# Dealing the routing of 24 token tiles to other places in a recurrence with a mixture of experts behind it

## The chip, the cores and the metric

One core of a Trainium2 chip runs the whole program. The metric is the device time of one execution in microseconds; the time of a kernel is the median of its runs.

## The reference, cut to what matters

A linear recurrence ("attention") runs over 4 batches, 8 heads, 768 positions and 48 channels; its output, 3072 rows of 384, goes into a layer of 8 experts with one expert for each row, and only for rows whose skip score is positive.

```python
for t in range(S):
    cur = einsum('bhd,bhe->bhde', u * k[t], v[t])
    y[t] = einsum('bhd,bhde->bhe', r[t], state + cur)
    state = w * state + einsum('bhd,bhe->bhde', k[t], v[t])
x = y.transpose(0, 2, 1, 3).reshape(3072, 384)
do = x @ w_skip > 0
logits = x[do] @ w_gate                  # 8 columns
e = argmax(logits);  g = max of softmax(logits)
out = x;  out[do] += g * (relu(x[do] @ w1[e]) @ w2[e])   # 384 -> 1024 -> 384
```

## The kernel before

The attention works on 24 tiles of 128 rows: two batches by 64 positions, twelve tiles for each pair of batches. A loop of 23 steps (`for n in range(NT - 1)`, L905) makes tile n+1 in step n. All engines execute in the order in which the program issues (the schedule is manual), so the order of the calls in the loop is the order of the work on each engine.

PE in step n: `scores(n + 1)` (L441, into ps_p), `across(n + 1)` (L527, the state's part, from sblk), `turn_k(n + 2)` (L454), `turn_x(n)` (L569, the finished tile transposed for the gate), route matmuls if any, `state(n + 1)` (L474), and `within(n + 1)` (L503), which needs the masked scores am. Every fourth step holds the gate's matmuls for four tiles (`gate_some`, L597, steps 3, 7, ..., 19; the step after it `gate_back`, L613), which give the logits lg.

DVE in step n: the two masks of the scores (L462, L463), then what the routes have for this step, then `prep_r` of tile n+3 (L411, L419) and, every fourth step, the decayed state sblk (L486) between these two. POOL multiplies the keys of tile n+3 (kd, L429) and, from step 7, makes the low half of a piece of the experts' weights (lo, L114); ACT casts its high half (hi, L113) and copies results out of PSUM. SP issues the loads (dm, vz, raw) and the stores of the finished tiles.

A *route* (L634, a generator) turns the logits of a group of tiles into places in the experts' lists. Its groups are tiles 0 to 7, 8 to 15, 16 to 19 and 20 to 23. Its stages, each up to a `yield`: the largest logit and the choice (L646 to L670, one-hot oh); the rank matmuls on PE (L673 to L683, with the running count `before`); the rank arithmetic (L708 to L731); the one-hot of the lane ol and of the slot oj (L778, L782; for the later groups ol alone, L737, with 128 elements for each tile); the values vl (L789 or L744: row id and gate weight in two parts); the matmuls that collect vl by ol into the lists (L796 or L750) and the additions to `lists`. A `yield` of 0 lets a tick take the next stage at any place; 1, 2 and 4 mark stages that begin with PE work, taken at one place in a step. After group 2, `gather` (L122, POOL) fetches the rows of expert 0's first 128 slots from the stored output. The gathered tiles have numbers of their own, and 0 and 8 are expert 0's: where a gather or an expert is spoken of, "tile 0" and "tile 8" are these.

How many stages a step takes is set by `tick`:

```python
tick((1, 1, 2)[n % 3] if n < EARLY else 3 if n < TE else 6)     # EARLY = 16, TE = 20
```

A group starts when its logits are there: group 1 in step 8, group 2 in step 16, group 3 in step 20 (steps 20 and later take further stages at their end, L937 to L942), group 4 behind the loop. Behind the loop stand the transposes of tile 0 (L145), the transposes and gate of the last tile (L569, L613, L581), the first half of expert 0 (`widen`, L194) and, woven into it, the route of group 4, the gather of tile 8, and then the other experts (L154, L164), which run to the end.

Of the kernel before, what the change touches and what calls it, by code (L numbers as in the profile page):

```python
# [9 lines left out]
F32 = mybir.dt.float32  # L10
F32R = mybir.dt.float32r
# [5 lines left out]
ALU = mybir.AluOpType  # L17
AX = mybir.AxisListType
# [3 lines left out]
N, DM, E, F = B * S, H * D, 8, 1024  # L22
P = 128
# [23 lines left out]
EARLY = 16  # L47
# [5 lines left out]
W_MIN, W_MAX = 0.8, 1.2  # L53
HUGE = 1e30
FIRST = 12
GROUPS = [(0, 8), (8, 16), (16, 20), (20, 24)]


@with_exitstack
def tile_wkv_moe(  # L60
# [11 lines left out]
    nc = tc.nc  # L72
# [171 lines left out]
    with ExitStack() as actx:  # L244
# [348 lines left out]
        def gate_some(n, k=GB):  # L593
            pg = ps_l[:, : k * C]
            for j in range(NCC):
                for c in range(2):
                    nc.tensor.matmul(  # L597
                        pg[c * C : (c + 1) * C, :],
                        wgp[:, j, c, :],
                        gts[0][:, j, c, :k, :].rearrange("p k t -> p (k t)"),  # L600
                        start=(j == 0),
                        stop=(j == NCC - 1),
                        skip_group_check=True,
                    )
            lt = turned_lg[n] = wk.tile([P, GB * C], F32, tag="lt", name=f"lt{n}", bufs=1)[:, : k * C]
            nc.scalar.copy(lt, pg)
# [25 lines left out]
        lists = cpool.tile([P, NV3, NJ, E], F32, name="lists")  # L632

        def route(g0, g1):  # L634
            n, late = g1 - g0, g0 >= EARLY
            rp = ps_l if g1 == NT else ps_r
            mine = rp[:, : NV3 * NSL]
            l8 = lg[:, g0:g1, 0:E]
# [3 lines left out]
            def small(tag, dt=F32, w=None, bufs=None):  # L642
                return sm.tile([P, n] if w is None else [P, n, w], dt, tag=tag, name=f"{tag}{g0}", bufs=bufs)
# [16 lines left out]
            df = small("df", w=E)  # L660
            nc.vector.tensor_tensor(df, l8, bc(mx), ALU.subtract)
            yield 0
            if not late:
                nc.scalar.activation(df, df, AF.Exp)
            nc.vector.tensor_tensor(eq[:, :, :E], eq[:, :, :E], rdo, ALU.mult)
            m2 = small("m2")
# [1 line left out]
            yield 0  # L668
            oh = small("oh", BF16, E)
            nc.vector.tensor_tensor(oh, eq[:, :, :E], bc(m2), ALU.is_equal)  # L670
            yield 4 if late else 1
            pr = rp[:, 256:]
            nc.tensor.matmul(pr[:, : n * E], tri, oh.rearrange(col), start=True, stop=False, skip_group_check=True)  # L673
# [8 lines left out]
            for j in range(1, n):  # L682
# [5 lines left out]
                    stop=(j == n - 1),  # L688
                    skip_group_check=True,
                )  # L690
            gw = small("gw")

            def weigh():
                nc.vector.tensor_reduce(gw, df, AX.X, ALU.add)  # L694
                nc.vector.tensor_scalar(gw, gw, 1e-9, None, ALU.add)

            if late:
                nc.scalar.activation(df, df, AF.Exp)
            else:
                weigh()  # L700
            yield 0
            rk = small("rkp", w=E)
            gh, gl = small("gh", F32R), small("gl", F32R)
            r1 = small("r1")
            sums = sm.tile([P, E], F32, tag="sums", name=f"sums{g0}")

            def ranks():
                nc.vector.tensor_tensor(rk, pr[:, : n * E].rearrange("p (n e) -> p n e", e=E), oh, ALU.mult)  # L708

            def count():  # L710
                nc.vector.tensor_reduce(sums, oh.rearrange("p n e -> p e n"), AX.X, ALU.add)

            if late:
                ranks()
# [21 lines left out]
            if late:  # L736
                nc.vector.tensor_tensor(  # L737
                    ol, lane1[:, None, :].to_broadcast([P, n, P]), r1.unsqueeze(2).to_broadcast([P, n, P]), ALU.is_equal
                )
                vl = small("vl", F32R, NV3 * E)  # L740

                def value(*qs):
                    for q in qs:
                        nc.vector.tensor_tensor(  # L744
                            vl[:, :, q * E : (q + 1) * E], oh, vals[q].to_broadcast([P, n, E]), ALU.mult
                        )

                def collect(v0, v1):
                    for j in range(n):
                        nc.tensor.matmul(  # L750
                            part[:, v0:v1, NJ - 1, :],
                            ol[:, j, :],
                            vl[:, j, v0 * E : v1 * E],
                            start=(j == 0),
                            stop=(j == n - 1),
                        )
                    into = lists[:, v0:v1, NJ - 1, :]
                    nc.vector.tensor_tensor(into, part[:, v0:v1, NJ - 1, :], into, ALU.add)

                value(0)  # L760
                yield 4
                collect(0, 1)
                if g1 == NT:
                    place_ids(1)
                yield 0
                weigh()
                nc.vector.reciprocal(gw, gw)
                nc.vector.tensor_copy(gh, gw)
                nc.vector.tensor_tensor(gl, gw, gh.bitcast(F32), ALU.subtract)
                value(1, 2)  # L770
                if g1 < NT:
                    count()
                    nc.vector.tensor_tensor(before, before, sums, ALU.add)
                yield 4
                collect(1, NV3)
                nc.vector.tensor_scalar(over[:, g0:g1], r1, float(CAP), None, ALU.is_ge)
                return
            nc.vector.tensor_tensor(  # L778
                ol, lane[:, None, :].to_broadcast([P, n, P]), lo.unsqueeze(2).to_broadcast([P, n, P]), ALU.is_equal
            )  # L780
            oj = small("oj", w=NSL)
            nc.vector.tensor_tensor(  # L782
                oj, blk[:, None, :].to_broadcast([P, n, NSL]), hi.unsqueeze(2).to_broadcast([P, n, NSL]), ALU.is_equal
            )
            nc.vector.tensor_tensor(before, before, sums, ALU.add)
            yield 0
            vl = small("vl", F32R, NV3 * NSL)
            for q, val in enumerate(vals):
# [21 lines left out]
        def place_ids(j):  # L810
            nc.vector.tensor_scalar(gid[:, j * E : (j + 1) * E], lists[:, 0, j], 1.0, 0.0, ALU.subtract, ALU.max)
# [6 lines left out]
            nc.vector.scalar_tensor_tensor(sid[:, c], ids, -1.0, em2, ALU.add, ALU.add)  # L818
            nc.vector.tensor_tensor(gate_s[:, c], lists[:, 1, j], lists[:, 2, j], ALU.add)

        ends = {g1: g0 for g0, g1 in GROUPS}
        routes = []

        def step_route(kind):
            if routes and routes[0][1] == kind and routes[0][2] < seen[0] + 2:
                k = next(routes[0][0], None)
                if k is None:
                    routes.pop(0)
                else:
                    routes[0][1] = k  # L830
                return True
            return False

        def tick(k=1):
            for _ in range(k):
                step_route(0)

        def both(g):
            for _ in g:
                pass  # L840
# [32 lines left out]
        def piece(j, split=False):  # L873
            e, j = divmod(j, NPC)
            if split:
                split_piece(e, j, nc.gpsimd)
            else:
                load_piece(e, j)
# [26 lines left out]
        for n in range(NT - 1):  # L905
            if n + 5 < NT:
                load_dm(n + 5)
            if n + 4 < NT and n:
                load_v(n + 4)
            scores(n + 1)  # L910
            mask_scores(n + 1)
            across(n + 1)
            if n >= FIRST_LOAD + LEAD:
                piece(n - FIRST_LOAD - LEAD, split=True)
            if 0 < n and n + 2 < NT:
                bonus(n + 2, BH)
            turn_k(n + 2)
            if 0 < n <= TE and n % GB == 0:
                gate_back(n - 1)
            turn_x(n)  # L920
            if n + 3 < NT:
                prep_k(n + 3)
            for kind in (1, 2, 4):
                step_route(kind)
            tick((1, 1, 2)[n % 3] if n < EARLY else 3 if n < TE else 6)
            if n + 3 < NT:
                prep_r(n + 3, (0,))
            back = state(n + 1)
            if n + 3 < NT:
                prep_r(n + 3, (1,))  # L930
            if n < TE and n % GB == GB - 1:
                gate_some(n)
            elif n == NT - 2:
                gate_some(n, NT - 1 - TE)
            within(n + 1, kcopy.get(n + 2, xcopy[n]))
            evac(n + 1)
            if back:  # L937
                back()
            if n >= TE:
                for kind in (1, 2, 4):  # L940
                    step_route(kind)
                tick()  # L942
            if n + 1 in ends:
                routes.append([route(ends[n + 1], n + 1), 0, n + 1])
            if 1 <= n < 5:
                next(setup, None)
            if n >= FIRST_LOAD:
                piece(n - FIRST_LOAD)
        done = NT - 1 - FIRST_LOAD - LEAD
        for j in range(done + LEAD, 2 * NPC):  # L950
            piece(j)
# [9 lines left out]
        turn_x(NT - 1)  # L961
        piece(done, split=True)
        gate_back(NT - 2, NT - 1 - TE)
        run(1)
        gate(NT - 1)
        last = route(ends[NT], NT)
        while next(last) == 0:
            pass
        run(2)
# [366 lines left out]
```

## Time and profile before

| | |
|---|---|
| median of 3 runs | 274.98 us (274.95 to 278.34) |
| the profiled execution, its own time | 276.32 us |
| its span, first to last instruction | 274.2 us, clock 0.998 |
| PE, DVE, ACT, POOL busy | 255.6, 183.2, 141.1, 131.4 us |
| chain that ended last, by engine | PE 82%, DVE 10%, ACT 3% |

The profile is one execution. Its parts used here are the table of stretches (busy time of each engine between two moments), the instructions of an engine in order of time, with the idle time ahead of each and what ended it in brackets, and the chain of waits that ended last. A line number in a row is that of the kernel before.

### The profile page before, as it was taken

The numbers are of one execution on the slowest core, as the hardware profiler recorded it, in microseconds if no ns is written. First come the engines' busy times: TensorE is split into PE (matmuls) and PEld (weight loads), VectorE is DVE, ScalarE is ACT, GpSimd is POOL, SyncE is SP. The second block draws the span as 40 slices with busy tenths as digits, with TensorE's granted clock in tenths as the row PEclk, the third lists the DMA queues.
The fourth block names the chain that finished last, engine by engine and source line by source line (L and its number), as shares of the span: only waits on it lengthen the run. The fifth ranks groups of instructions, "written<-read, shape, count | busy, mean of one in ns | idle before, by whom it ended". The sixth has DMA issues, their size and how long they took to land.

```text
span 274.2 us, 8740 instructions
## 1 busy us (share of the span) xinstructions
PE 255.6 (93%) x3545; PEld 233.9 (85%) x3545; DVE 183.2 (67%) x372; ACT 141.1 (51%) x316; POOL 131.4 (48%) x131
## 2 busy tenths in 40 slices
PE   7998999999979989788999999999999999999990
PEld 2797897878869877776879999999999999999990
DVE  8786657598896899954655686757748377483310
ACT  2664566667756756434455554717548085480300
POOL 8536313375545538511748853763525535255011
PEclk9999999999999999999999999999999999999999
DMA  7977678878999995435479994694837747100010
GB/s 201 308 197 240 163 203 277 248 247 256 289 274 282 272 284 159 114 93 143 111 254 308 365 379 166 219 317 145 260 121 241 241 142 261 43 4 27 15 35 23
DMA packets 31140, 54.30 MB, mean 198 GB/s; under 512 B 4535, under 2 KB 14412, under 8 KB 31088
## 3 DMA queue, kind: packets, MB, share of 16 engines
q1 hardware_dynamic: 28896, 48.19, 57.2%
q0 software_dynamic: 2048, 5.44, 5.8%
q8 instruction: 30, 0.49, 0.7%
q14 instruction: 22, 0.18, 0.2%
q10 hardware_dynamic: 144, 0.00, 0.0%
HBM read 45.82 MB, written 8.65 MB: 199 GB/s over the span
## 4 chain that ended last, share of the span: by engine, by line
PE 82%; DVE 10%; ACT 3%; issue 2%; DMA 1%; POOL 0%; POOLq 0%; ACTq 0%
PE ps_p L164 11%; PE ps_y L164 11%; PE ps_p L441 8%; PE ps_p L154 5%; PE ps_r L154 5%; PE ps_l L154 5%; PE ps_y L154 5%; PE ps_s L474 5%; PE ps_y L503 5%; PE ps_l L454 4%; PE ps_y L527 3%; PE ps_l L597 3%; PE ps_t L569 3%; PE ps_y L216 2%; PE ps_p L216 2%
## 5 line engine op out<-in xcount | busy, mean ns | idle before, releaser
L114 POOL TENSOR_TENSOR lo<-raw,hi 128x512 fp32r<-128x512 f32 x42 | 57.0, 1358 | 75.3 <-ACT hi L113 55.7
L113 ACT CAST hi<-raw 128x512 fp32r<-128x512 f32 x96 | 55.1, 624 | 0.0
L114 DVE TENSOR_TENSOR lo<-raw,hi 128x512 fp32r<-128x512 f32 x54 | 44.0, 837 | 2.6 <-ACT hi L113 2.3
L429 POOL TENSOR_TENSOR kd<-dm,w_d 128x512 f32<-128x512 f32 x22 | 30.1, 1366 | 14.7 <-DMA dm<-in_dm_dram 13.0
L172 POOL DMA_INDIRECT out_dram<-xg,sid x16 | 17.1, 1067 | 36.4 <-DVE xg L169 25.7
L462 DVE COPY_PREDICATED am<-below,ps_p 128x512 f32<-128x512 int8 x24 | 17.7, 739 | 17.1 <-PE ps_p L441 17.0
L441 PE MATMUL ps_p<-rd,kd 64*64 64x128 f32 x768 | 26.9, 276 | 0.3 <-issue 0.3
L441 PEld LDWEIGHTS ps_p<-rd,kd 64*64 64x64 f32 x768 | 20.9, 132 | 3.2 <-issue 0.7
L158 ACT ACTIVATE hh<-ps_p 128x464 fp32r<-128x464 f32 x7 | 3.9, 559 | 36.9 <-PE ps_p L154 20.1
L122 POOL DMA_INDIRECT xg<-out_dram,gid x16 | 18.2, 1139 | 8.7 <-DVE gw L694 4.0
L503 PE MATMUL ps_y<-vz,am 128*64 128x96 f32 x384 | 20.2, 247 | 2.1 <-DVE am L463 1.5
L503 PEld LDWEIGHTS ps_y<-vz,am 128*64 128x64 f32 x384 | 17.8, 137 | 3.4 <-issue 1.9
L405 ACT ACTIVATE rd<-rd,uw 128x128 f32<-128x128 f32 x52 | 17.8, 395 | 4.9 <-DVE rd L411 4.9
L474 PE MATMUL ps_s<-vz,kt 128*64 128x96 f32 x352 | 19.6, 253 | 0.0
L456 ACT COPY kt<-ps_l 128x512 f32<-128x512 f32 x22 | 12.8, 583 | 12.9 <-PE ps_l L454 12.9
L164 PE MATMUL ps_p<-hi,hh 128*128 128x384 f32 x56 | 19.4, 347 | 0.0
L164 PE MATMUL ps_y<-hi,hh 128*104 128x384 f32 x56 | 18.9, 338 | 0.0
L164 PE MATMUL ps_p<-hi,hl 128*128 128x384 f32 x56 | 18.9, 337 | 0.0
L164 PE MATMUL ps_y<-lo,hh 128*104 128x384 f32 x56 | 18.9, 337 | 0.0
L164 PE MATMUL ps_y<-hi,hl 128*104 128x384 f32 x56 | 18.9, 337 | 0.0
L164 PE MATMUL ps_p<-lo,hh 128*128 128x384 f32 x56 | 18.8, 336 | 0.0
L169 DVE SCALAR_TENSOR_TENSOR xg<-ps_y,gate_s,xg 104x384 f32<-104x384 f32 (+1 forms) x8 | 4.9, 616 | 20.5 <-PE ps_y L164 17.9
(244 smaller groups left out, 693.4 us busy)
## 6 DMA issues: line engine op xcount, KB each, us to landing
raw<-in_w_dram SPq DMA_DIRECT2D x96, 256.0 KB
dm<-in_dm_dram SPq DMA_DIRECT2D x24, 512.0 KB
vz<-in_tok_dram SPq DMA_DIRECT2D x48, 96.0 KB
out_dram<-xt SPq DMA_DIRECT2D x48, 96.0 KB
out_dram<-xt SPq DMA_DIRECT2D x4, 192.0 KB
xg<-out_dram,gid POOLq DMA_INDIRECT x16
out_dram<-xg,sid POOLq DMA_INDIRECT x16
wgp<-in_wgq_dram SPq DMA_DIRECT2D x1, 192.0 KB
```

The lines of the kernel that those rows point to most:

```text
L113: nc.scalar.copy(hi, t)
L114: eng.tensor_tensor(lo, t, hi.bitcast(F32), ALU.subtract)
L122: ins = nc.gpsimd.indirect_dma_start(out=xg, out_offset=None, in_=out[0:rows], in_offset=bass.IndirectOffsetOnAxis(ap=gid[:, q : q + 1], a ...
L154: nc.tensor.matmul(ph, a[:, c, fs], b[:, c, :], start=(k == 0), stop=(k == 3 * NCC - 1))
L164: nc.tensor.matmul(py, a, b[:, f, :], start=(k == 0), stop=(k == 3 * NFC - 1))
L172: ins = nc.gpsimd.indirect_dma_start(out=out, out_offset=bass.IndirectOffsetOnAxis(ap=sid[:, q : q + 1], axis=0), in_=xs.pop(q), in_offset ...
L405: nc.scalar.mul(rd[:, :, 1], rd[:, :, 0], uw[:, hp : hp + 1])
L429: (eng or nc.gpsimd).tensor_tensor(kds[n], d[:, 1], w_d[:, n % NSUB, 1][:, :, None].to_broadcast([DR, NHP, 2, C]), ALU.mult,)
L441: nc.tensor.matmul(ps_p[q * C : (q + 1) * C, a, 2 * hp * C : 2 * (hp + 1) * C], kd[h, hp, q, :], rd[h, hp, q].rearrange("p s c -> p (s c)" ...
L462: nc.vector.copy_predicated(shape(am[n % 2]), below, p[:, :, 0])
L474: nc.tensor.matmul(s[a * C : (a + 1) * C, :, hp * D : (hp + 1) * D], kt[:, hp, a, :], t[:, :, a, hp, :], start=i == 0 and hp == 0, stop=Tr ...
L503: ins = nc.tensor.matmul(place_y(a, c)[:, :, g, :], am[n % 2][:, a, hp * C : (hp + 1) * C], t[:, :, a, hp, :], start=g == 0 and n % NSTEP ...
```

## The change

A table, DEAL, now gives the number of stages for each step; steps that are not in it take none. In the route of the first two groups the slot one-hot oj comes in a stage of its own ahead of the lane one-hot ol. Group 3 (`mid`) leaves the loop's list of routes: its choice, gate weights and counts are issued at the end of step 22, its rank matmuls, ranks, ol and vl behind the gate's `gate_back` after the loop, and its collecting matmuls, three lists at once, after the gate of the last tile, ahead of group 4. The stages at the end of steps 20 and later are gone. Line numbers of the changed kernel are higher by 1 to 12 in these parts.

```diff
+DEAL = {8: 2, 9: 2, 10: 1, 11: 1, 12: 1, 13: 1, 15: 2, 16: 4, 17: 2, 19: 2, 20: 2}
...
         def route(g0, g1):
-            n, late = g1 - g0, g0 >= EARLY
+            n, late, mid = g1 - g0, g0 >= EARLY, EARLY <= g0 and g1 < NT
...
-            if not late:
+            if not late or mid:
                 nc.scalar.activation(df, df, AF.Exp)
...
             nc.vector.tensor_tensor(oh, eq[:, :, :E], bc(m2), ALU.is_equal)
+            if mid:
+                weigh()
+                part_weight()
+                count()
             yield 4 if late else 1
...
                 value(0)
+                if mid:
+                    value(1, 2)
+                    nc.vector.tensor_tensor(before, before, sums, ALU.add)
+                    nc.vector.tensor_scalar(over[:, g0:g1], r1, float(CAP), None, ALU.is_ge)
+                    yield 4
+                    collect(0, NV3)
+                    return
...
-            nc.vector.tensor_tensor(
-                ol, lane[:, None, :].to_broadcast([P, n, P]), lo.unsqueeze(2).to_broadcast([P, n, P]), ALU.is_equal
-            )
             oj = small("oj", w=NSL)
             nc.vector.tensor_tensor(
                 oj, blk[:, None, :].to_broadcast([P, n, NSL]), hi.unsqueeze(2).to_broadcast([P, n, NSL]), ALU.is_equal
             )
             nc.vector.tensor_tensor(before, before, sums, ALU.add)
             yield 0
+            nc.vector.tensor_tensor(
+                ol, lane[:, None, :].to_broadcast([P, n, P]), lo.unsqueeze(2).to_broadcast([P, n, P]), ALU.is_equal
+            )
+            yield 0
...
-        ends = {g1: g0 for g0, g1 in GROUPS}
+        ends = {g1: g0 for g0, g1 in GROUPS if g1 <= EARLY}
+        mid = route(*GROUPS[2])
...
-            tick((1, 1, 2)[n % 3] if n < EARLY else 3 if n < TE else 6)
+            tick(DEAL.get(n, 0))
...
             elif n == NT - 2:
                 gate_some(n, NT - 1 - TE)
+                while next(mid) == 0:
+                    pass
             within(n + 1, kcopy.get(n + 2, xcopy[n]))
...
-            if n >= TE:
-                for kind in (1, 2, 4):
-                    step_route(kind)
-                tick()
...
         gate_back(NT - 2, NT - 1 - TE)
+        while next(mid) == 0:
+            pass
         run(1)
         gate(NT - 1)
-        last = route(ends[NT], NT)
+        both(mid)
+        last = route(*GROUPS[3])
```

What the edits do to the order is shown at three places. The first is DVE from the masks of step 13 on (am is written by the masks, rd by prep_r, sblk by the state's decay). Before:

```order
L462 COPY_PREDICATED am_151<-below,ps_p 128x512
L463 COPY_PREDICATED am_151<-eye,ps_p 128x512
L778 TENSOR_TENSOR ol_1431<-lane,lo_1343 128x1024
L782 TENSOR_TENSOR oj_1433<-blk,hi_1248 128x128
L785 TENSOR_TENSOR before<-before,sums_1243 128x8
L411 TENSOR_TENSOR rd_1436<-dm_1189,w_d 128x8x64
L419 TENSOR_TENSOR rd_1436<-rd_1436,uw 128x4x64
L462 COPY_PREDICATED am_152<-below,ps_p 128x512
L463 COPY_PREDICATED am_152<-eye,ps_p 128x512
L789 TENSOR_TENSOR vl_1517<-oj_1433,id_195 128x8x16
```

Now, from behind the same masks of step 13:

```order
L790 TENSOR_TENSOR oj_1432<-blk,hi_1248 128x128
L793 TENSOR_TENSOR before<-before,sums_1095 128x8
L412 TENSOR_TENSOR rd_1435<-dm_1208,w_d 128x8x64
L420 TENSOR_TENSOR rd_1435<-rd_1435,uw 128x4x64
L463 COPY_PREDICATED am_152<-below,ps_p 128x512
L464 COPY_PREDICATED am_152<-eye,ps_p 128x512
L412 TENSOR_TENSOR rd_1516<-dm_1285,w_d 128x8x64
L487 TENSOR_TENSOR sblk_199<-ps_s,pw 128x384
L420 TENSOR_TENSOR rd_1516<-rd_1516,uw 128x4x64
L463 COPY_PREDICATED am_151<-below,ps_p 128x512
L464 COPY_PREDICATED am_151<-eye,ps_p 128x512
L795 TENSOR_TENSOR ol_1431<-lane,lo_1343 128x1024
```

The lane one-hot of group 1 stood in step 13 ahead of rd and of the next step's masks; it now stands behind the masks of step 15, with the three vl behind it. Group 2's ol moved from step 19 to step 20 in the same way.

The second place is PE in step 21, from its scores to the next step's. Before:

```order
L441 MATMUL ps_p<-rd_1997,kd_1986 64x128 x16
L527 MATMUL ps_y<-sblk_199,rd_1997 64x48 x16
L569 MATMUL ps_t<-ident,xt_2139 128x128 x3
L750 MATMUL ps_r<-vl_2159,ol_2157 128x8 x4
L474 MATMUL ps_s<-vz_130,kt_2073 64x2x48 x8
L503 MATMUL ps_y<-vz_130,am_151 64x2x48 x8
L750 MATMUL ps_r<-vl_2159,ol_2157 128x2x8 x4
L441 MATMUL ps_p<-rd_2119,kd_2083 64x128 x16
```

Now:

```order
L442 MATMUL ps_p<-rd_1992,kd_1979 64x128 x16
L528 MATMUL ps_y<-sblk_199,rd_1992 64x48 x16
L570 MATMUL ps_t<-ident,xt_2105 128x128 x3
L806 LDWEIGHTS ones
L806 MATMUL ps_r<-before,ones 128x8
L808 MATMUL ps_r<-vl_2081,ol_1988 128x48 x8
L475 MATMUL ps_s<-vz_130,kt_2068 64x2x48 x8
L504 MATMUL ps_y<-vz_130,am_151 64x2x48 x8
L442 MATMUL ps_p<-rd_2085,kd_2078 64x128 x16
```

Both collects of group 3 (L750) left the step; the collect of group 2, which stood in step 20, is here instead.

The third place is DVE behind the loop (xhl is the low half of tile 0, rkp and r the ranks, mx the start of group 4's route). Before:

```order
L463 COPY_PREDICATED am_152<-eye,ps_p 128x512
L147 TENSOR_TENSOR xhl_2324<-ps_s,xhl_2324 128x384
L646 MEMSET eq_2353 128x4
L648 TENSOR_REDUCE mx_2355<-lg 128x4
L650 SCALAR_TENSOR_TENSOR rdo_2357<-lg,rev 128x32
```

Now:

```order
L148 TENSOR_TENSOR xhl_2297<-ps_s,xhl_2297 128x384
L721 TENSOR_TENSOR rkp_2321<-ps_r,oh_2257 128x32
L725 TENSOR_REDUCE r_2322<-rkp_2321 128x4
L747 TENSOR_TENSOR ol_2325<-lane_193,r_2322 128x512
L754 TENSOR_TENSOR vl_2327<-oh_2257,id_195 128x4x8
L754 TENSOR_TENSOR vl_2327<-oh_2257,gh_2260 128x4x8
L754 TENSOR_TENSOR vl_2327<-oh_2257,gl_2261 128x4x8
L773 TENSOR_TENSOR before<-before,sums_2262 128x8
L774 TENSOR_SCALAR over<-r_2322 128x4
L768 TENSOR_TENSOR lists<-ps_r,lists 128x3x8
L647 MEMSET eq_2348 128x4
L649 TENSOR_REDUCE mx_2350<-lg 128x4
```

Nine instructions of group 3 stand between tile 0's low half and group 4's first reduction; the last of them, the addition to the lists, is behind four matmuls of PE (L760), which PE has after the gate of the last tile (L582).

More of the change, by code (lines that the diff above doesn't have):

```diff
@@ L670, in route, with weigh, part_weight, count @@
             nc.vector.tensor_tensor(oh, eq[:, :, :E], bc(m2), ALU.is_equal)
+            gw = small("gw")
+            gh, gl = small("gh", F32R), small("gl", F32R)
+            sums = sm.tile([P, E], F32, tag="sums", name=f"sums{g0}")
+            def weigh():
+                nc.vector.tensor_reduce(gw, df, AX.X, ALU.add)
+                nc.vector.tensor_scalar(gw, gw, 1e-9, None, ALU.add)
+            def part_weight():
+                nc.vector.reciprocal(gw, gw)
+                nc.vector.tensor_copy(gh, gw)
+                nc.vector.tensor_tensor(gl, gw, gh.bitcast(F32), ALU.subtract)
+            def count():
+                nc.vector.tensor_reduce(sums, oh.rearrange("p n e -> p e n"), AX.X, ALU.add)
+            if mid:
+                weigh()
+                part_weight()
+                count()
             yield 4 if late else 1
@@ L690, in route @@
                 )
[L691 to L697, printed above, removed]
+            if late and not mid:
                 nc.scalar.activation(df, df, AF.Exp)
-            else:
+            elif not late:
                 weigh()
@@ L702, in route @@
             rk = small("rkp", w=E)
-            gh, gl = small("gh", F32R), small("gl", F32R)
             r1 = small("r1")
-            sums = sm.tile([P, E], F32, tag="sums", name=f"sums{g0}")
             def ranks():
                 nc.vector.tensor_tensor(rk, pr[:, : n * E].rearrange("p (n e) -> p n e", e=E), oh, ALU.mult)
-            def count():
-                nc.vector.tensor_reduce(sums, oh.rearrange("p n e -> p e n"), AX.X, ALU.add)
             if late:
@@ L760, in route @@
                 value(0)
+                if mid:
[5 more added lines that the diff above has]
+                    return
                 yield 4
                 collect(0, 1)
-                if g1 == NT:
-                    place_ids(1)
+                place_ids(1)
                 yield 0
                 weigh()
-                nc.vector.reciprocal(gw, gw)
-                nc.vector.tensor_copy(gh, gw)
-                nc.vector.tensor_tensor(gl, gw, gh.bitcast(F32), ALU.subtract)
+                part_weight()
                 value(1, 2)
-                if g1 < NT:
-                    count()
-                    nc.vector.tensor_tensor(before, before, sums, ALU.add)
                 yield 4
@@ L948, in tile_wkv_moe @@
                 piece(n - FIRST_LOAD)
+        assert not routes
         done = NT - 1 - FIRST_LOAD - LEAD
```

## The prediction

> **What bounds the kernel now.** I read the table of stretches first, cut at the first score matmul (L441) of each step: step n runs from scores(n+1) to scores(n+2), so 71.23 us opens step 13 and 118.99 us step 22; the last two long rows are the stretch behind the attention and the experts. A row gives length, then busy time (and instructions) of PE, weight load, DVE, ACT and POOL, the clock, the DMA share and GB/s.
>
> ```profile
> 53.99:71.23 17.24, 16.23 (x385) 14.16 (x385) 15.36 (x32) 11.94 (x29) 10.24 (x8) 1.00 0.85 260
> 71.23:75.10 3.87, 3.87 (x105) 3.53 (x103) 3.16 (x5) 3.04 (x7) 2.54 (x2) 1.00 0.90 259
> 75.10:80.71 5.61, 4.09 (x105) 3.60 (x103) 5.54 (x11) 2.54 (x6) 3.18 (x2) 1.00 0.92 279
> 80.71:86.68 5.97, 5.97 (x125) 5.33 (x123) 4.52 (x8) 3.81 (x9) 2.53 (x2) 1.00 0.96 291
> 86.68:91.54 4.86, 4.45 (x110) 4.01 (x108) 3.43 (x10) 3.44 (x9) 2.52 (x2) 1.00 0.85 256
> 91.54:95.41 3.87, 3.87 (x106) 3.53 (x104) 3.30 (x6) 3.04 (x7) 2.53 (x2) 1.00 0.97 289
> 95.41:99.50 4.09, 4.09 (x115) 3.88 (x113) 3.82 (x10) 2.56 (x6) 2.53 (x2) 1.00 0.97 290
> 99.50:106.34 6.84, 5.67 (x118) 4.57 (x116) 6.74 (x16) 3.85 (x9) 3.50 (x2) 1.00 0.86 244
> 106.34:112.78 6.44, 5.63 (x124) 5.31 (x122) 6.11 (x24) 3.33 (x8) 4.04 (x3) 1.00 0.35 90
> 112.78:118.99 6.21, 4.87 (x111) 4.19 (x107) 5.63 (x18) 3.36 (x9) 1.70 (x1) 1.00 0.41 108
> 118.99:123.38 4.39, 3.82 (x96) 3.30 (x96) 1.71 (x4) 1.11 (x3) 1.27 (x1) 1.00 0.42 108
> 123.38:144.18 20.80, 19.25 (x119) 15.60 (x117) 10.97 (x38) 9.86 (x25) 9.86 (x9) 1.00 0.57 171
> 144.18:268.00 123.82, 123.78 (x906) 122.02 (x904) 73.92 (x119) 59.21 (x118) 58.65 (x48) 1.00 0.54 181
> 71.23:99.50 28.27, 26.34 (x654) 23.88 (x652) 23.78 (x46) 18.42 (x44) 15.83 (x12) 1.00 0.93 278
> ```
>
> PE sets the end. From 144.18 us it works 123.78 of 123.82 us at full clock, so the experts can't shrink, only start earlier. Before them a step without route work takes 3.87 us (steps 13 and 17). Steps 14 and 19 to 21 have PE idle, and there DVE is the fullest engine (5.54 of 5.61, 6.74 of 6.84, 6.11 of 6.44, 5.63 of 6.21). Next I read PE's order of time for what ends those idles (the bracket: idle time before the row, and its releaser).
>
> ```profile
> 60.58 0.88 PE L503 MATMUL ps_y<-vz,am 128*64 128x96 f32 x16 [0.54 <-ACT kt L456]
> 79.90 0.88 PE L503 MATMUL ps_y<-vz,am 128*64 128x96 f32 x16 [1.52 <-DVE am L463]
> 101.77 0.81 PE L527 MATMUL ps_y<-sblk,rd 64*64 64x48 f32 x32 [1.17 <-DVE sblk L486]
> 112.58 0.18 PE L673 MATMUL ps_r<-oh,tri 128*128 128x32 bf16 x1 [0.40 <-DVE oh L670]
> 115.86 0.61 PE L750 MATMUL ps_r<-vl,ol 128*128 128x8 f32 x4 [1.06 <-DVE vl L744]
> 118.45 0.61 PE L750 MATMUL ps_r<-vl,ol 128*128 128x16 f32 x4 [0.20 <-DVE vl L744]
> ```
>
> All come from route work in front of something PE needs: the masked scores (am) at 79.90, the decayed state (sblk) at 101.77, the route's own operands in steps 20 and 21. The cause of the longest is in DVE's and POOL's rows.
>
> ```profile
> 73.67 1.30 POOL L429 TENSOR_TENSOR kd<-dm,w_d 128x512 f32<-128x512 f32 x1
> 73.81 2.24 DVE L778 TENSOR_TENSOR ol<-lane,lo 128x1024 fp32r<-128x1024 f32 x1
> 79.65 0.28 DVE L789 TENSOR_TENSOR vl<-oj,id 128x128 fp32r<-128x128 f32 x1
> 79.84 0.29 DVE L789 TENSOR_TENSOR vl<-oj,gh 128x128 fp32r<-128x128 f32 x1
> 113.95 0.69 DVE L737 TENSOR_TENSOR ol<-lane,r 128x512 fp32r<-128x512 f32 x1
> 114.06 1.70 POOL L114 TENSOR_TENSOR lo<-raw,hi 128x512 fp32r<-128x512 f32 x1 [1.34 <-ACT hi L113]
> 114.56 1.25 DVE L744 TENSOR_TENSOR vl<-oh,id 128x32 fp32r<-128x32 bf16 x1
> ```
>
> The lane one-hot ol starts beside POOL's kd (over at 74.97) and ends at 76.05, 1.08 us after it: it hardly advanced meanwhile. In the last two rows a vl of 32 elements takes 1.25 us and ends at 115.81, just behind POOL's 115.76. The two engines exclude each other here.
>
> **Steps 9 to 12.** The first group's rank matmuls move from step 11 to step 10. They cost 0.22 us, the excess of step 18 (4.09) over step 17 (3.87), and in step 10 stand in the 0.54 us that PE waits for kt: -0.2.
>
> **Steps 13 to 18.** The ol leaves step 13; step 14 loses its wait and falls from 5.61 to 3.87: -1.74. The lists' matmuls (L796) go from step 15 to 16, the second ranks from 18 to 17: no net change. What the eight list matmuls cost a step is read from the chain of waits, where each stands with the time that it alone takes; the second row has the small matmul of the last table in it.
>
> ```profile
> 83.18 0.81 PE ps_r L796 x8
> 109.80 0.93 PE ps_r L796 x8
> ```
>
> Steps 14 to 18 become 3.87+5.16+5.67+4.09+3.87: 0.81 off step 15's 5.97 and on step 16's 4.86, 0.22 off step 18 and on step 17.
>
> ol and its three vl now stand in steps 15 and 20. An ol cost a plain step 1.52 us of waiting; three vl, 0.19 from one start to the next, bring that to 2.1. Step 15 is 1.29 longer than a plain one by its own gate matmuls, and step 16 by 0.99 and 0.81 more, before within() needs the mask: nothing is left. Step 20 is 0.99 longer (4.86 against 3.87), and step 21 gets L796 (0.9) ahead of its within(): 0.2 left. Step 17 carries the whole rank arithmetic in a plain step: 0.3, by the way DVE's 3.82 of 4.09 us in step 18 just fit. Together **+0.5**; from 0 up to 1.5, one whole wait as in step 14.
>
> **Steps 19 to 21.** Group three and its PE work are gone. Step 19 becomes a step like 15 without L796: 5.16 for 6.84, -1.68. Step 20 becomes a step like 16: 4.86 for 6.44, -1.58 (L796 0.93 with the small matmul ahead, ranks 0.22, wait 0.40). Step 21 loses two L750 of 0.54, waits of 1.06 and 0.20, some 0.4 of refilling PE behind them, and gains L796 at 0.93: 6.21 to 4.45, -1.76. Step 22 keeps 4.39: DVE is busy 1.71 us there, so group three's one-hots and weights run beside PE. Sum of the attention: -0.2-1.74-1.68-1.58-1.76 = **-6.96**.
>
> **Behind the attention** the third group's ranks, ol, vl and collect now stand between PE's transposes of tile 0 and the last group's route.
>
> ```profile
> 123.38 0.55 PE L145 MATMUL ps_s<-ident,xg 128*128 128x128 f32 x3
> 124.91 0.50 PE L194 MATMUL ps_p<-hi,xhl 128*128 128x512 f32 x1
> 125.74 1.27 POOL L114 TENSOR_TENSOR lo<-raw,hi 128x512 fp32r<-128x512 f32 x1 [5.09 <-ACT hi L113]
> 125.81 0.87 PE L581 MATMUL ps_y<-wgp,xT 128*64 128x18 f32 x12
> 126.92 0.19 DVE L648 TENSOR_REDUCE mx<-lg 128x4 f32<-128x32 f32 x1 [1.81 <-ACT lg L588]
> 128.11 0.19 PE L673 MATMUL ps_l<-oh,tri 128*128 128x32 bf16 x1
> 128.43 0.19 DVE L708 TENSOR_TENSOR rkp<-ps_l,oh 128x32 f32<-128x32 f32 x1 [0.42 <-PE ps_l L683]
> 128.87 0.69 DVE L737 TENSOR_TENSOR ol<-lane,r 128x512 fp32r<-128x512 f32 x1
> ```
>
> PE's share is ranks 0.2 and one collect of four matmuls 0.55. DVE has 1.81 us free before 126.92, and the chain would just fit: the last group's runs rkp to ol in 0.44, ol to its end in 0.69. Ranks at 124.9, where PE starts the first half of expert 0 now (L194), put rkp at 125.2 and ol at 125.65 to 126.3. But POOL's lo starts at 125.74, so the pair of 113.95 and 114.06 repeats: lo waits for ol, then all vl wait for lo, and are done at about 127.7 (115.81 is 1.86 us behind the ol's start; 125.65+1.86, and two more vl). PE has finished the gate (L581 ends 126.68, some 0.2 later now) and waits 0.9, then collects; DVE adds the lists and starts mx at 128.4 instead of 126.92. The last group's ranks follow at 129.8 for 128.11. All that stands behind them (its ol, gather of tile 8, expert 0's second half) moves alike, since PE is busy 19.25 of these 20.80 us. **+1.7**; 0.8 without the block, 2.0 if lo comes first.
>
> [...]
>
> **The gather of tile 0** comes out of step 21 now, not step 20.
>
> ```profile
> 111.46 1.26 POOL L122 DMA_INDIRECT xg<-out_dram,gid  x1 [1.15 <-DVE em L817]
> 131.01 1.02 POOL L122 DMA_INDIRECT xg<-out_dram,gid  x1 [4.00 <-DVE gw L694]
> 137.09 0.49 PE L145 MATMUL ps_t<-ident,xg 128*128 128x128 f32 x3
> ```
>
> Before, it had 11.92 us until L145 used it. Now L796 ends 2.9 us into step 21, the list arithmetic follows the masks (to 3.75, if the ol of step 20 makes them a microsecond late), and six small DVE operations put the issue some 0.7 behind that: 4.45. Steps 21 and 22 last 8.84, so the lead is 4.4 us. Tile 8's gather needed at most 6.08 us (131.01 to 137.09, no wait ahead of L145), and above zero: a wait of 0 to 1.7. I take **+0.2**, near no wait, because nothing says that the 6.08 were used up and the DMA share here is 0.42.
>
> [...]
>
> **Sum.** -6.96+0.5+1.7+0.2 = -4.56. The profiled execution took 276.32 us around a span of 274.2; it becomes 271.8. The median of the runs is 274.98, 1.34 less for the same kernel; with the same difference it becomes **270.4**, 1.7% faster. The best ends (0, 0.8, 0) give 268.8, the worst (1.5, 2.0, 1.7) 273.2.
>
> **Rivals.** (1) Everything hides: POOL's lo comes clear of the chain, no mask is late. For it: DVE's 1.81 us gap behind the attention. Against: 125.65 against 125.74. -6.96+0.8: **268.8**, over 2% faster.
>
> (2) The loads hold steps 13 to 18. For it: from 71.23 to 99.50 us the DMA share is 0.93 at 278 GB/s. The same bytes in 26.53 us need 296 GB/s, and the best attention row has 291; the loads are issued for a pace that the steps then beat. Against: at 291 GB/s they take 27.0 us, a loss of 0.5, and from step 20 on the share is 0.35 to 0.42, so lateness is absorbed. If the old pace stays, 1.74 is lost: **272.2**.
>
> (3) Slower than before: the gather lands late, PE stands in order at the first L145, and every later piece of expert 0 waits with it. Each us beyond the 4.4 us lead costs one; the gain is gone at 9.0 us. The trace allows at most 11.92 for this transfer, at which the time is 270.2+11.92-4.4 = **277.7**. Against it: tile 8's 6.08.
>
> **How the numbers follow.** The forecast has 0.55, from 269.5 to 271.7 us. Rival 1 has 0.25, rival 2 0.17, rival 3 0.03. 2% of 274.98, about what a measurement of this kernel can tell from no change, lies at 269.5 and 280.5: faster 0.25 is rival 1; within 2% 0.73 holds the forecast, rival 2 and rival 3 up to its bound; slower 0.02, for something that no row shows. The range 268.6 to 272.6 takes in rivals 1 and 2 and leaves out rival 3 and the joint worst ends.
>
> **What would show it.** In the changed profile: step 14 at 3.9 us with no wait for am; steps 19 to 21 at 5.2, 4.9 and 4.5; scores(23) to scores(10) about 6.5 us closer. Behind the attention, a first vl (now L754) of over 1 us beside POOL's lo, a PE wait of 0.9 ahead of the collect (L760), and the stretch from the first transposes of tile 0 to expert 1 at about 22.5 instead of 20.80. A wait ahead of those transposes means the gather; DMA waits ahead of rd, kd or hi in steps 13 to 18 mean rival 2. An attention that keeps more than 2 us of waits in steps 14 to 21, or a stretch behind it over 24 us, makes the forecast wrong.

## The result, and the profile after

The change takes **274.01 us** (median of 20 runs, 272.54 to 279.66) against 276.71 (20 runs of the kernel before beside it): ratio **0.9895**, 95% interval 0.9871 to 0.9919. A repeat gave 274.27 (12 runs) against 275.90 (29): 0.9974 (0.9939 to 1.0009). Ratios and intervals leave out the runs that are more than 1.5% above the fastest of their kernel, a slower state; medians and ranges take in all runs. So the change is worth about 1% in the first comparison and 0.3%, not told from nothing, in the second: within 2%. The forecast, 270.4 with 268.6 to 272.6 around it, was too low. The profiled execution went from 276.32 to 274.07 us, by 2.25 instead of 4.56, and 0.69 of that is code ahead of step 9 that the change leaves alone.

The first row is steps 9 to 22 of the kernel before. The others are the changed kernel: the same steps together, then steps 10, 14, 15, 16 and 19 to 22, then the stretch behind the attention and the experts (columns as in the prediction; PE is TensorE, DVE is VectorE, ACT is ScalarE, POOL is GpSimd):

```profile
53.92:123.38 69.46, 62.63 (x1476) 55.49 (x1475) 59.40 (x135) 42.00 (x101) 36.59 (x27) 1.00 0.77 227
53.23:118.45 65.22, 61.64 (x1464) 54.23 (x1462) 55.98 (x120) 42.26 (x101) 35.86 (x27) 1.00 0.82 241
56.87:62.04 5.17, 3.59 (x99) 3.34 (x97) 5.00 (x12) 2.66 (x6) 2.77 (x3) 1.00 0.92 278
75.72:79.59 3.87, 3.87 (x105) 3.54 (x103) 3.78 (x7) 2.56 (x6) 2.54 (x2) 1.00 0.86 243
79.59:85.14 5.55, 5.54 (x117) 4.44 (x115) 5.52 (x7) 3.81 (x9) 3.52 (x2) 1.00 0.97 293
85.14:90.81 5.67, 5.26 (x118) 4.95 (x116) 4.27 (x17) 3.43 (x9) 2.78 (x3) 1.00 0.88 245
98.76:104.48 5.72, 5.72 (x117) 4.57 (x115) 5.62 (x14) 3.94 (x9) 2.52 (x2) 1.00 0.84 251
104.48:109.34 4.86, 4.45 (x110) 4.01 (x108) 4.19 (x6) 3.23 (x8) 2.52 (x2) 1.00 0.64 164
109.34:113.69 4.35, 4.35 (x111) 4.13 (x109) 3.65 (x13) 2.65 (x6) 2.20 (x2) 1.00 0.53 140
113.69:118.45 4.76, 4.07 (x98) 3.30 (x96) 2.63 (x11) 1.93 (x5) 1.87 (x2) 1.00 0.53 138
118.45:141.71 23.26, 21.27 (x127) 17.07 (x126) 14.64 (x53) 9.86 (x25) 10.34 (x9) 0.93 0.51 151
141.71:265.60 123.89, 123.77 (x906) 122.00 (x904) 76.19 (x120) 59.32 (x118) 58.47 (x48) 1.00 0.55 182
```

Steps 9 to 22 got shorter by 4.24 us (69.46 to 65.22) where 6.46 were forecast, the tail behind them got longer by 2.46 where 1.7 were, and the experts stayed. (The prediction's table opens step 9 at 53.99 us; PE's first L441 row begins at 53.92, so its first row is 0.07 too short.) Step 10 is the surprise, 5.17 for 3.82. This is how it begins on DVE and POOL in the kernel before, from the end of step 9 on:

```profile
56.35 1.29 POOL L429 TENSOR_TENSOR kd<-dm,w_d 128x512 f32<-128x512 f32 x1
56.50 1.22 DVE L665 TENSOR_TENSOR eq<-eq,rdo 128x64 f32<-128x64 f32 x1
58.62 0.42 DVE L419 TENSOR_TENSOR rd<-rd,uw 128x256 f32<-128x256 f32 x1
58.77 1.40 POOL L114 TENSOR_TENSOR lo<-raw,hi 128x512 fp32r<-128x512 f32 x1 [1.13 <-PE ps_p L441]
```

And in the changed kernel, with the masks and PE behind it:

```profile
55.66 1.30 POOL L430 TENSOR_TENSOR kd<-dm,w_d 128x512 f32<-128x512 f32 x1
55.80 1.24 DVE L666 TENSOR_TENSOR eq<-eq,rdo 128x64 f32<-128x64 f32 x1
57.34 0.22 DVE L671 TENSOR_TENSOR oh<-eq,m 128x64 bf16<-128x64 f32 x1
57.48 0.68 DVE L412 TENSOR_TENSOR rd<-dm,w_d 128x512 f32<-128x512 f32 x1
58.07 1.28 POOL L115 TENSOR_TENSOR lo<-raw,hi 128x512 fp32r<-128x512 f32 x1 [1.11 <-PE ps_p L442]
58.20 1.43 DVE L420 TENSOR_TENSOR rd<-rd,uw 128x256 f32<-128x256 f32 x1
60.31 0.73 DVE L464 COPY_PREDICATED am<-eye,ps_p 128x512 f32<-128x512 int8 x1
61.14 0.97 PE L504 MATMUL ps_y<-vz,am 128*64 128x96 f32 x16 [1.58 <-issue]
```

DVE is blocked twice. The first block, of L666 by POOL's kd (1.24 us for 64 elements, where `e1_early` below has 0.21), is in the kernel before too (L665, 1.22). New is L671, which the table moved from step 10 into step 9: behind it, L420 starts 0.13 us after POOL's lo, where it started 0.15 us ahead of it, and is blocked as well (1.43 us for 0.42). The masks end at 61.04 and PE, idle for 1.58 us, starts at 61.14. ("issue" only says that the profile names no releaser.)

In the tail, the forecast block of the first vl (1.25 us, the two vl behind it 0.18 each) and the wait ahead of the collect of group 3 (1.00 us) are there:

```profile
120.81 1.75 POOL L115 TENSOR_TENSOR lo<-raw,hi 128x512 fp32r<-128x512 f32 x1 [4.05 <-ACT hi L114]
121.35 1.25 DVE L754 TENSOR_TENSOR vl<-oh,id 128x32 fp32r<-128x32 bf16 x1
122.86 0.61 PE L760 MATMUL ps_r<-vl,ol 128*128 128x24 f32 x4 [1.00 <-DVE vl L754]
```

What was not forecast is the clock behind that wait (half-microsecond stretches, the clock before the DMA share):

```profile
123.50:124.00 0.50, 0.50 (x3) 0.42 (x3) 0.49 (x6) 0.00 (x0) 0.00 (x0) 1.00 0.44 115
124.00:124.50 0.50, 0.50 (x4) 0.35 (x3) 0.44 (x4) 0.00 (x0) 0.00 (x0) 0.70 0.72 197
127.00:127.50 0.50, 0.50 (x4) 0.50 (x3) 0.00 (x0) 0.00 (x0) 0.00 (x0) 0.50 0.00 0
127.50:128.00 0.50, 0.50 (x5) 0.50 (x5) 0.09 (x1) 0.00 (x0) 0.00 (x0) 0.89 0.00 0
```

TensorE was granted half its clock from about 124.2 to 127.6 us. No wait stands ahead of the first transposes of tile 0 (118.45): the gather was in time.

The code ahead of step 9, which the change leaves alone, ends between 52.3 and 55.1 us in the profiled executions. These 2.7 us belong to no edit, so the experiments below are read by stretches first: **attention** is steps 9 to 22, **tail** the stretch from there to expert 1.

### The profile page after: what moved, and what is told of

The parts are those of the page before. It is cut to its first block, busy times and chain, and to the rows that moved or that the text cites. A ratio compares the mean times of both kernels' runs of the same rounds, so it can differ in the third digit from the quotient of the medians.

```text
span 272.1 us, 8730 instructions
## 1 busy us (share of the span) xinstructions
PE 255.9 (94%) x3540; PEld 233.5 (86%) x3541; DVE 185.9 (68%) x371; ACT 141.5 (52%) x316; POOL 131.1 (48%) x131
## 4 chain that ended last, share of the span: by engine, by line
PE 69%; ACT 2%; DVE 2%; issue 2%; DMA 1%; POOL 0%; POOLq 0%; SPq 0%; ACTq 0%
PE ps_p L165 11%; PE ps_y L165 11%; PE ps_p L155 5%; PE ps_r L155 5%; PE ps_l L155 5%; PE ps_y L155 5%; PE ps_p L442 4%; PE ps_y L504 3%; PE ps_s L475 3%; PE ps_l L455 2%; PE ps_l L598 2%; PE ps_y L528 2%; PE ps_t L570 2%; PE ps_y L217 2%; PE ps_p L217 2%
## 5 line engine op out<-in xcount | busy, mean ns | idle before, releaser
L114 ACT CAST hi<-raw 128x512 fp32r<-128x512 f32 x96 | 55.1, 624 | 0.0
L115 DVE TENSOR_TENSOR lo<-raw,hi 128x512 fp32r<-128x512 f32 x54 | 45.9, 873 | 2.6 <-ACT hi L114 2.3
L412 DVE TENSOR_TENSOR rd<-dm,w_d 128x512 f32<-128x512 f32 x24 | 19.4, 810 | 0.0
```

Of the source, the lines that this page charges most:

```text
L114: nc.scalar.copy(hi, t)
L115: eng.tensor_tensor(lo, t, hi.bitcast(F32), ALU.subtract)
L412: nc.vector.tensor_tensor(rds[n][:, :, :, 0], d[:, 0], w_d[:, n % NSUB, 0][:, :, None].to_broadcast([DR, NHP, 2, C]), ALU.mult,)
```

## The experiments

**Step 10** (`e1_early`).

```diff
-DEAL = {8: 2, 9: 2, ...
+DEAL = {8: 3, 9: 1, ...
```

> The table's first rows become 8: 3, 9: 1 (two segments more stand in step 8 up to the second maximum, one in step 9; the rank matmuls stay in step 10). My theory: step 10 grew from 3.82 to 5.17 us because the masks of that step start late on VectorE, which GpSimd blocked twice, in the L666 of step 9 (1.24 us in place of 0.2) and, half a microsecond later than it could have been, in the L420 (1.43 in place of 0.43). With L666 and L668 gone from step 9 the L420 ends ahead of GpSimd's next piece, step 10 takes about 3.85 us, the attention is 1.3 us shorter and the kernel takes about 272.7 us in place of 274.0. Rival: the eight rank matmuls and the weight sums put into step 10 hold it by themselves; then step 10 stays at 5.1 to 5.2 and the time at 274.0.

Step 10 took 3.62 us; 273.78 us (12 runs), 0.9906 (0.9868 to 0.9944). The time of the whole kernel, expected at 272.7, does not show the gain; the step does.

```profile
57.17 1.29 POOL L430 TENSOR_TENSOR kd<-dm,w_d 128x512 f32<-128x512 f32 x1
58.47 0.68 DVE L412 TENSOR_TENSOR rd<-dm,w_d 128x512 f32<-128x512 f32 x1
59.19 0.43 DVE L420 TENSOR_TENSOR rd<-rd,uw 128x256 f32<-128x256 f32 x1
59.60 1.28 POOL L115 TENSOR_TENSOR lo<-raw,hi 128x512 fp32r<-128x512 f32 x1 [1.13 <-PE ps_p L442]
```

L420 now starts 0.41 us ahead of POOL's lo and takes 0.43. The rank matmuls still stand in step 10, so they were not the cause. One small DVE operation too many in step 9 cost 1.35 us against the kernel before. This doesn't depend on the execution: the six profiles with the change's first rows have step 10 at 5.07 to 5.17 us, the ten with 8: 3, 9: 1 at 3.62 to 3.97.

**Steps 15 and 19** (`e3_swap`).

```diff
-            if n + 3 < NT:
-                prep_r(n + 3, (0,))
             back = state(n + 1)
+            if n + 3 < NT:
+                prep_r(n + 3, (0,))
```

> The changed kernel with the state's matmuls and its scaling (L487 on VectorE in steps 14 and 18, which starts the next pair of steps) issued ahead of the L412 of the same step. My theory: steps 15 and 19 are 0.39 and 0.56 us over their forecast because L487 stands behind an L412 that GpSimd's kd blocks for 1.7 us; with L487 ahead, step 15 takes 5.2 and step 19 5.2, and the kernel about 273.1 us. Rival: L487 waits for the state's matmuls itself and holds L412, and so the next step's first products, up by as much; then the two steps gain nothing and others lose 0.2 to 0.5: 274.0 to 274.6.

Both steps took 5.31 us; 274.02 us (6 runs), 0.9836 (0.9773 to 0.9899): the whole time, expected at 273.1, shows nothing clear. In the changed kernel and then in this one, DVE at the end of step 14:

```profile
78.31 1.69 DVE L412 TENSOR_TENSOR rd<-dm,w_d 128x512 f32<-128x512 f32 x1
79.93 0.55 DVE L487 TENSOR_TENSOR sblk<-ps_s,pw 128x384 f32<-128x384 f32 x1
```

```profile
79.93 0.56 DVE L487 TENSOR_TENSOR sblk<-ps_s,pw 128x384 f32<-128x384 f32 x1 [0.69 <-PE ps_s L475]
80.40 0.68 DVE L412 TENSOR_TENSOR rd<-dm,w_d 128x512 f32<-128x512 f32 x1
```

The equal 79.93 is a coincidence: step 15 begins at 79.59 in the one and at 80.40 in the other, so the state comes 0.81 us sooner. The blocked L412 was worth 0.24 us in step 15, and as much in step 19 when that is taken from the repeat of the change (5.54 there, 5.72 in its first profile). The 0.15 that both still have over the forecast has another cause, which no run shows.

**The tail's wait** (`e6_pool`: the lo of that piece on VectorE, ahead of the collect; `e2_warm`: the wait filled).

```diff
-        piece(done, split=True)
+        de, dj = divmod(done, NPC)
+        dt = raw.pop((de, dj))
+        dhi, dlo = (b[de % 2][:, dj * QC : (dj + 1) * QC] for b in (his, los))
+        nc.scalar.copy(dhi, dt)
...
         gate(NT - 1)
+        nc.vector.tensor_tensor(dlo, dt, dhi.bitcast(F32), ALU.subtract)
         both(mid)
```

> The changed kernel with the one lo piece that GpSimd makes in the tail (120.81 to 122.56 us) made on VectorE instead, behind the over of tiles 16 to 19 and ahead of the addition to the lists (L768). My theory: that piece blocks the first vl (L754, 1.25 us in place of 0.18), and TensorE waits 1.00 us for it ahead of L760, and this wait brings the clock of 0.50 behind it. Both go: L760 follows L582 at once, the addition is 0.9 us sooner, the clock stays at 1.00, the tail is 21.5 to 21.9 us in place of 23.26, and the kernel takes about 272.4 us. Rival: the wait goes and the clock falls all the same, since the matmuls around it are too small to count: then 273.1 to 273.3 us. Second rival: VectorE's piece (0.6 us) is in the way of L768 and takes back most of it: 273.6.

Tail 21.34 us, clock 1.00; 272.53 us (6 runs), 0.9867 (0.9822 to 0.9911).

```diff
         gate(NT - 1)
+        warm(4)
         both(mid)
```

> The changed kernel with four filler matmuls of ones (128x512, bf16, into a bank that nobody reads then) between the last gate's matmuls (L582) and the collect matmuls (L760), where TensorE is idle for 1.00 us. My theory: the granted clock of 0.50 from 124.1 to 127.5 us follows from that idle; with the gap filled the clock stays at 1.00 there, the tail behind the attention is 22.4 to 22.6 us in place of 23.26, and the kernel takes about 273.2 us. Rival: the clock falls whatever TensorE does in that microsecond (the other small matmuls around it count for nothing either); then clock and tail stay, and the time is 274.0 to 274.2.

Tail 22.43 us, clock 1.00; 272.33 us (6 runs), 0.9884 (0.9837 to 0.9932). But `e1_early` and `e3_swap`, whose tail is the change's, also kept the clock: 22.38 and 22.41 us. So the wait costs 1.05 us by itself, and whether the clock falls differs from execution to execution, which one profile cannot tell.

**The two parts alone.** `e4_tail_only` deals tiles 0 to 15 as before (with ol and oj in one stage again), `e5_table_only` takes the table for tiles 0 to 7 alone and leaves tiles 16 to 19 in the attention.

```diff
...
-            tick(DEAL.get(n, 0))
+            tick((1, 1, 2)[n % 3] if n < EARLY else 3 if n < TE else 6)
```

> One part of the change alone: tiles 16 to 19 routed behind the attention as in the change, the routes of tiles 0 to 15 dealt to the steps as before (and ol with oj in one step). My theory after the first runs: the table's gains (ol out of step 13) and its loss (step 10) cancel over steps 9 to 18, 45.5 us in both kernels, so that all of the change's gain comes from this part. Steps 9 to 18 take 45.5 +-0.3, step 20 about 4.9 in place of 6.44, step 21 about 4.4 in place of 6.21, the tail 22.4 in place of 20.8; the kernel 1.8 to 3.0 us under the one before. Rival: without the table the ol and vl of tiles 8 to 15 stay in step 19 at 6.4 to 6.8 us and lose half of it: 0.8 to 1.5 us under before.

275.55 us (12 runs), 1.0009 (0.9967 to 1.0050): no gain shown, where the rival had 0.8 to 1.5 us. Steps 9 to 18 took 45.56, as expected, but steps 19 and 20 stayed long, as the rival said (its rows: steps 19 and 20, attention, tail):

```profile
98.80:105.64 6.84, 5.67 (x117) 4.57 (x116) 6.74 (x16) 3.86 (x9) 3.52 (x2) 1.00 0.87 258
105.64:111.41 5.77, 5.36 (x118) 5.04 (x116) 5.52 (x16) 3.33 (x8) 3.44 (x3) 1.00 0.46 119
53.24:119.46 66.22, 61.37 (x1464) 54.28 (x1462) 55.80 (x120) 42.14 (x101) 36.37 (x27) 1.00 0.80 236
119.46:143.67 24.21, 22.59 (x127) 18.59 (x126) 14.36 (x53) 9.86 (x25) 9.83 (x9) 0.86 0.52 157
```

The attention is 3.24 us shorter than in the kernel before, and the tail, with the low clock, 3.41 longer.

```diff
...
-            tick((1, 1, 2)[n % 3] if n < EARLY else 3 if n < TE else 6)
+            tick(DEAL.get(n, 0) if n < EARLY else 3 if n < TE else 6)
```

> The other part alone: in the kernel before, the route of tiles 0 to 7 dealt to steps 8 to 15 by the change's table, with ol in a step of its own; from step 16 on all as before, tiles 16 to 19 within the attention. My theory: step 10 takes 5.1 to 5.2 in place of 3.82, step 14 3.87 in place of 5.61, step 15 5.55 in place of 5.97; the rest stays; the kernel is 0.5 to 0.9 us under the one before (no measurable change). Rival, the prediction's reading: the table is worth its 1.7 us in steps 13 to 15 with no loss elsewhere, 2.0 to 2.3 us under before.

276.31 us (12 runs), 1.0008 (0.9975 to 1.0041); attention 69.55, tail 20.81, nothing gained. Steps 14 (4.69, not the 3.87 expected) and 15 (5.31) give 1.58 us; steps 10 (5.15) and 16 (5.66, it now has the list matmuls, which the expectation forgot) take 2.13. The late rows of the table (steps 16 to 20) stand in neither part. Moving tiles 16 to 19 alone leaves step 19 at 6.84; with the late rows as well, it is 5.72 in the change. Neither part pays alone in these runs.

**The change again** (`e8_change_again`).

> The changed kernel once more, unaltered, for a second look at two places of its profile. My theory: the clock of 0.50 behind the 1.0-us wait in the tail and the 4.76 of step 22 belong to single executions: with the same wait, two other kernels kept the clock at 1.00 and had a tail of 22.4 us and a step 22 of 4.39. So the tail is 22.4 (clock 1.00) in most executions, 23.3 in some, and step 22 is 4.39; the median is 272.5 to 274.0. Rival: both belong to this kernel's order, and the profile shows them again: tail 23.2 to 23.3, step 22 about 4.75.

Step 22 took 4.38, so its 4.76 is not in every execution; but the tail was 23.58, again with a clock of 0.50 for 3.4 us. So the theory was right on step 22 and wrong on the tail. (The long step 22 comes back, at 4.76 to 4.80, in `e14_wait_back`, `e15_fill_again` and `e16_fill_both`.)

**All three edits** (`e9_all`).

> The changed kernel with the three edits together: the table's first rows 8: 3, 9: 1; the state ahead of L412; the tail's lo piece on VectorE. If the three act in different places they add up: step 10 3.65 (-1.5), steps 15 and 19 5.31 each (-0.25 each), tail 21.35 (-1.05 against a tail with the clock at 1.00): 3.0 us under the changed kernel, 270.0 to 271.2 us, 0.977 to 0.982 of before. Rival: the loads (DMA share 0.86 to 0.97 in steps 13 to 18) then arrive too late for the shorter steps and hold one of steps 15 to 19 back by 0.5 to 1.5 us: 271.2 to 272.5.

271.34 us (6 runs), 0.9859 (0.9819 to 0.9899):

```profile
53.57:116.35 62.78, 60.79 (x1464) 54.05 (x1462) 53.02 (x119) 41.76 (x100) 35.49 (x27) 1.00 0.84 250
116.35:137.70 21.35, 19.82 (x128) 16.20 (x126) 14.11 (x54) 9.85 (x25) 8.60 (x8) 1.00 0.55 164
```

In this profile they add up. The time, a little over the 270.0 to 271.2 expected, is below that of the change in the same series (269.60 to 272.42 against 273.02 to 277.02 in `e8_change_again`). Run again (`e17_all_again`) it gave 272.21 us, 0.9824 (0.9781 to 0.9868), a tail of 21.31, but an attention of 65.69. Late loads, the rival, are at least a part of that (see the rivals below).

**What brings the low clock.** `e10_attention` has the first two edits alone; `e12_gap2` makes the wait longer; `e14_wait_back` puts one into `e9_all` with VectorE's work alone; `e15_fill_again` is `e11_attention_fill` once more, which is `e10_attention` with the wait filled. `e11_attention_fill` took 273.83 us; four of its six runs have a low clock, where a quarter was expected, and its profile shows it too, 6.5 us behind the wait.

> The changed kernel with the two edits in the attention alone (table rows 8: 3, 9: 1; the state ahead of L412); the tail as the change has it, with TensorE's wait of 1.00 us. My theory: the attention is 2.0 us shorter than the change's, and the clock falls to 0.50 in the tail in about half of the executions (it did in three of the five profiled ones that have this wait, in none of the four without it), for one or two stretches of 3.4 us, at 0.9 to 1.8 us each time. So of the runs about half have a mean clock of 0.991 or less, and the median is 272.2 to 273.2 us, 1 to 2 us behind the kernel with all three edits. Rival: the clock in the tail has nothing to do with the wait; then as many runs are over 0.991 as with the wait filled.

274.80 us (12 runs), 0.9923 (0.9882 to 0.9964); tail 25.77 us, clock 0.50 for 10.2 us. The median is over the 272.2 to 273.2 expected; of the runs 8 of 12 have a low clock, where about half was expected.

```diff
         piece(done, split=True)
+        piece(done + 1, split=True)
...
-        piece(done + 1, split=True)
```

> As e10_attention, with GpSimd's second lo piece of the tail issued right behind the first, so that VectorE's vl, and TensorE behind it, wait for both: a wait of 2.2 to 2.9 us in place of 1.00. My theory: the longer wait brings the clock of 0.50 in nearly every execution (three quarters of the runs or more at 0.991 or less), and the tail is 1.2 to 1.9 us longer by the wait and again 0.9 to 1.8 by the clock: 24.5 to 26.1 us, the kernel 2 to 3 us over e10_attention. Rival: VectorE slips its three vl in between the two pieces; then the wait stays at 1.0, and time and clock are those of e10_attention.

275.90 us (12 runs), 0.9943 (0.9895 to 0.9991); wait 2.06 us, tail 25.22.

```diff
+                for _ in range(3 if mid else 1):
                     nc.vector.tensor_tensor(ol, ...
```

> The kernel with all three edits (e9_all), in which VectorE makes the lane one-hot of tiles 16 to 19 (L747) three times over, so that TensorE again waits some 1.1 to 1.2 us ahead of the collect, without a GpSimd piece there. My theory, that idleness brings the low clock: at least half of the runs have a mean clock of 0.991 or less, and the median is 1.5 to 2.5 us over e17_all_again (1.2 by the wait, the rest by the clock). Rival, that the GpSimd piece or the filled attention brings it: as few low clocks as in e17_all_again, and 1.1 to 1.3 us over it.

274.78 us (10 runs), 0.9909 (0.9871 to 0.9947):

```profile
119.13 2.14 DVE L748 TENSOR_TENSOR ol<-lane,r 128x512 fp32r<-128x512 f32 x3
121.63 0.61 PE L761 MATMUL ps_r<-vl,ol 128*128 128x24 f32 x4 [1.38 <-DVE vl L755]
```

> e11_attention_fill once more, unaltered (wait of 1.00 us filled with four matmuls of ones). If the filling cures the low clock, under a quarter of the runs have 0.991 or less, and the median is about 1.1 us over e17_all_again; if it doesn't, half or more have, and the median is 1.8 to 2.5 over it.

272.81 us (6 runs), 0.9873 (0.9836 to 0.9910). Each run has a mean granted clock on record. In the 18 profiles, those at 0.990 or less are the ones with the low clock in the tail, so runs at 0.991 or less are counted as low:

| TensorE's wait ahead of the collect of group 3 | low, of all runs |
|---|---|
| none (before, e5, e6, e9, e13, e17) | 18 of 120 |
| 1.0 us (the change, e8, e1, e3, e4, e10) | 53 of 74 |
| 1.4 us (e14), 2.1 us (e12) | 10 of 10, 12 of 12 |
| 1.0 us, filled (e2, e11, e15, e16) | 6 of 24 |

e14 has no GpSimd piece at that place and a low clock in all 10 runs, so in this tail TensorE's idleness brings the low clock, not the block. Filling the wait helps (6 of 24 low, where 53 of 74 were), but not always: e11 and e15, the same kernel, have 4 of 6 and none of 6. Filling the 0.5 us wait ahead of the next collect as well showed nothing more: `e16_fill_both` 272.30 us, and `e13_all_fill`, on top of `e9_all`, 272.01, tail 21.37.

## Why the prediction was wrong, point by point

- **Steps 9 to 12** is the step that failed. The prediction costed the move of stages into steps 9 and 10 by the matmuls alone (-0.2). Measured: +1.31 (17.31 to 18.62), of which step 10 is 1.35; step 11 took 4.90 for 4.93, so the 0.2 did not come either. DVE's small operations were put at nothing; where they stand against POOL's two pieces of each step was not asked, though the prediction had read that exclusion elsewhere (1.25 us for a vl of 32 elements). `e1_early` shows that this, and not the matmuls, made step 10 long.
- **Steps 13 to 18**: step 14 at 3.87, 16 at 5.67, 17 and 18 at 4.08 and 3.87 are as forecast. The 0.5 of lateness came as 0.39, all in step 15. The size is luck: the reason given was ol and vl ahead of the masks, but 0.24 of it is L412 ahead of the state (`e3_swap`).
- **Steps 19 to 22**: 20 and 21 (4.86, 4.35 for 4.86, 4.45) are right, 19 was 0.56 too long (0.18 less in `e8_change_again`), 22 by 0.37 in this profile and three others. The 0.4 of refilling PE in the sum of step 21 was the author's estimate: no run shows it as such, only the step at 4.35. Step 22 has this row:

```profile
114.40 0.48 ACT L539 COPY xt<-ps_y 128x384 f32<-128x384 f32 x1 [0.72 <-DMA out_dram<-xt]
```

  The profile says that this copy waits for a store, which would free its buffer. In the other three the same 0.7 us stands ahead of it, put down to PE. No run tests it, so the cause stays open.
- **The miss of the attention** is 2.22 us, to 0.02: 1.35 step 10, 0.17 step 11, 0.39 and 0.56 steps 15 and 19, 0.37 step 22, less 0.5 allowed and 0.1 in step 21. With two of these put right `e9_all` has 62.78 us, where the forecast's own terms give 63.00. But that is the best of nine profiles with this attention (`e9_all` to `e17_all_again`), which go up to 65.78 and have 63.55 in the middle.
- **The tail**: +1.7 was right at full clock (22.38 and 22.41 for 20.80), its block and its wait too (1.00 us for 0.9). No run shows the 2.0 taken for lo first: in the change ol starts at 120.74, lo behind it at 120.81. The clock was not in the sum; it adds 0.9 (23.26), and up to 3.4 (25.77 in `e10_attention`).
- **The gather**: issued at 113.04 us, 5.4 ahead of its use, and no wait; 0.2 too much.
- **The base**: the sum was made on 276.32 and moved to a median of three runs, 274.98; over 20 runs the median is 276.71, so 1.73 of the 3.61 us between forecast and result are the base. The forecast for the profiled execution itself was 271.8 for 274.07.
- **Rivals**: "everything hides" and the late gather did not happen. Late loads are not in the two profiles of the change, but they are in `e2_warm`, whose attention is the same (step 19 at 6.46 us), and in faster versions; in `e13_all_fill` step 16 takes 6.81 us for 5.67. In both ACT stands at a weight piece, here `e2_warm` first:

```profile
100.11 0.62 ACT L114 CAST hi<-raw 128x512 fp32r<-128x512 f32 x1 [1.25 <-DMA raw<-in_w_dram]
87.68 0.62 ACT L114 CAST hi<-raw 128x512 fp32r<-128x512 f32 x1 [1.63 <-DMA raw<-in_w_dram]
```

  `e17_all_again` has a wait of this kind too (0.78 us, in a step 20 of 5.15), but its longest loss, step 13 at 4.81 for 3.87, shows none. How often late loads cost time, and so their share of the medians, is not shown.

## What to carry to other kernels

Where two engines exclude each other, a small operation costs what it waits for and what its lateness makes wait next (here 0.22 us of L671 in step 9 put L420 at 1.43 us for 0.42, and step 10 at 5.17 for 3.82): lay moved work over the other engine's pieces by the times of the trace, not by the free share of a step. Take the base of a forecast from the execution that the sum is made on, when the median comes from three runs. A wait of the matmul engine can also have a price behind itself, in its clock (here 0.9 us of the tail's 23.26, and 3.4 of 25.77); count that over many runs, and move the work that makes it wait.

## What the hardware showed that was not expected

In this tail, an idle time of 1.0 us can be enough for half the clock. Of eight profiled executions with an unfilled wait of 1.0 us or more six show it, at 0.50, for one, two or three times 3.4 us (3.4 twice, 6.8 three times, 10.2), beginning between the wait itself and 1.8 us behind it. The length of the wait alone doesn't decide: 1.52 us in step 14 of the kernel before and 1.58 us in step 10 of the change left the clock at 1.00, in these steps and in the next. What sets the tail apart, where small matmuls and transposes stand around the wait, is not shown.
